# Recalibrating the planner of a static schedule: attention and a gated FFN on one core, with the softmax's exponentials shared by two engines

## The chip, the core and the metric

The kernel runs on one core of a Trainium2 chip. The core has five engines that run side by side, each through its own list of instructions in order: TensorE (PE, matrix products), ScalarE (ACT, here the exponentials), VectorE (DVE, elementwise work), GpSimd (POOL) and SyncE (SP, which here only issues DMA transfers). They tell each other of finished work through semaphores. Matrix products land in PSUM, which has eight banks of 128 x 512 float32; everything else lies in SBUF. The metric is the time of one execution on the device, in microseconds; the median of several runs is given.

## The reference

One transformer block with attention and FFN in parallel on the normalised input: 2048 positions, width 512, 32 heads of 16, FFN width 1792.

```python
x = A_x
xn = _layernorm(x, axis=-1)
return x + _A_ref(xn, A_wqkv, A_wo) + _B_ref(xn, B_w1, B_w3, B_w2)

# _A_ref: attention, Dh = 16
scores = jnp.einsum("bhqd,bhkd->bhqk", q, k) * (Dh ** -0.5)
p = _softmax(scores, axis=-1)
o = jnp.einsum("bhqk,bhkd->bhqd", p, v)
return (lambda x, *d: x.transpose(*d))(o, 0, 2, 1, 3).reshape(B, S, D) @ wo

# _B_ref: gated FFN
h = _silu(gate) * up
out = jnp.einsum("bsf,fd->bsd", h, w2)
```

With 32 heads of 16, the scores have 32 x 2048 x 2048 elements for little matrix work, so the exponentials are the large item.

## The kernel before

**Units, ranks, chunks.** Attention is cut into 32 units (`NU`): four blocks of 512 queries times eight groups of four heads. A unit has 64 ranks (`RPU`): 16 key tiles of 128 times four heads. Scores are made two ranks at a time, that is in chunks of 128 x 1024, 32 to a unit and 1024 in all (`score`, L1673: two matmuls that use two of the array's four row groups).

**Two ways to an exponential.** A chunk goes to ACT or to DVE. On ACT it is one instruction (`try_a`, L1716): exp from PSUM banks 0 and 1, or 2 and 3, into one of ten slots of PT. On DVE (`try_d`, `chain`) it goes by integer arithmetic on the bits of a bfloat16. p1 (L1768) clamps the scores of banks 4 and 5 into a slot of y as int16. Then, for one chunk or a pair of chunks together, m (L1807) takes the mantissa, g (L1823) subtracts a constant, t (L1814) multiplies y by m, and e (L1828) masks y in place. The exponential is the sum of e, g and t, and it is P·V that adds them: a DVE chunk gives three P·V terms where an ACT chunk gives one. There are three slots of y, two of m (t overwrites m) and two of g. A slot comes free when P·V has read it.

**P·V and dense work.** P·V (`try_pv`, L1882) works in column mode, four heads side by side, and adds into bank 7 for one unit at a time, in the order of the units. When a unit is complete, DVE copies bank 7 out (`unit_end`, L1900) and a small chain of DMAs and DVE or POOL work normalises it. Everything else on PE is "dense" work in column mode: projections, FFN and output (L1301), in tiles that use bank 6 alone in the long middle stage. Each FFN tile needs ACT for a tanh (L1462) and DVE for two products (L1466, L1476).

**The planner.** No order is written by hand. `_plan_fast` runs a small event simulation in Python when the kernel is built. Time `P.t` goes on in steps of 0.02 us; at each step every free engine takes the posted piece with the lowest priority number whose time has come (`post`, `pump`), and PE takes the first that fits of: a chunk for ACT, a chunk for DVE, dense work (while the P·V backlog is under `PVQ` tasks), P·V, dense work. What it takes is appended to that engine's list, and those lists are the program. The durations are formulas (`a_cost`, `d_cost`, `s_cost`, and numbers at single pieces); a result counts as ready `_LAT` after its end. So the share of chunks that DVE gets, and all order, come from the model's times. On the chip only the order and the semaphores remain: an engine waits until its next instruction's inputs are there, whatever the planner thought.

**Dependencies.** `_collect` finds, by keys, what an instruction must wait for: the last writer of what it reads, and the last writer and the readers of what it writes. `_finish` drops those on PE itself; on DVE and ACT an instruction does wait, by semaphore, for an earlier one of its own engine. The slots of y, m and g lie where x was, so p1, m and g name all 16 keys of x (`XD`) among their writes.

**DVE chunks at a unit's end.** `try_d` takes the next rank in order. It takes none past rank 52 of a unit (`D_LAST`), and past rank 42 (`D_PAIR`) it makes chains of one chunk. Ranks go alternately to the two halves of the row groups (`dpar`). p1 of the next pair waits until the chain before has done two of its four steps (first chunk) or four (second).

Of the kernel before, what the change touches and what calls it, by code (L numbers as in the profile page):

```python
# [20 lines left out]
class _Prog:  # L21
# [7 lines left out]

    def _collect(self, op, reads, writes):  # L30
# [22 lines left out]
        deps.pop(id(op), None)  # L53
        return list(deps.values())
# [15 lines left out]
    def op(self, eng, fn, reads=(), writes=(), name="", first=None):  # L70
# [7 lines left out]
        deps = self._collect(op, reads, writes)  # L78
        return self._finish(op, deps)
# [58 lines left out]
_LAT = 0.09  # L138


class _Sched(_Prog):


    def __init__(self):
# [5 lines left out]
        self.ring = 0.0  # L150

    def _time(self, op, deps, dur, tail):
        ready = self.t
# [5 lines left out]
        start = max(self.free[op.eng], ready)  # L159
        op.end = start + dur + tail  # L160
        self.free[op.eng] = start + dur
        return op

    def op(self, eng, fn, reads=(), writes=(), dur=0.1, name=""):
        op = _Prog.op(self, eng, fn, reads, writes, name)
        return self._time(op, op.deps, dur, 0.18 if eng == "pe" else 0.0)
# [828 lines left out]
def _plan_fast(nc, ps, flag, A_x, A_wqkv, A_wo, B_w1, B_w3, B_w2, out):  # L995
# [18 lines left out]
    NP = NG // 2  # L1014
    NY = 3
    NM = 2
# [5 lines left out]
    D_PAIR = RPU - 22  # L1022
    D_LAST = RPU - 12
    NW = 3
    PVQ = 8
# [10 lines left out]
    with ctx:  # L1036
# [59 lines left out]
        XD = [("x", t) for t in range(NT)]  # L1096
        def xk(s0, n):
# [86 lines left out]
        def norm(t):  # L1184
# [4 lines left out]
                     reads=[("x", t), ("lnr", n0), ("mv", t)], writes=[("xn", xs)], dur=0.25)  # L1189
# [4 lines left out]
        def stat(ts, prio):  # L1194
# [3 lines left out]
            def one(t):  # L1198
                nrm0[t] = t0
                P.op("dve", lambda e: e.bn_stats(stats[:, t, :], x_sb[:, t, :]),  # L1200
                     reads=[("x", t)], writes=[("st", t)], dur=0.64)
# [45 lines left out]
        P.post("dve", wv_check, ready=60.0, prio=4)  # L1247

        def tail_consts():
# [15 lines left out]
            P.post("dve", tail_masks, ready=P.free["pool"] + _LAT, prio=4)  # L1265
# [303 lines left out]
        st = {"dbl": 0, "pos": 0, "pv": 0, "dpar": 0, "nd": 0, "lastA": -1.0, "n_exp": 0, "pm": ("col", None, 0.0)}  # L1569
# [74 lines left out]
        def pe_dur(mode, rows=None):  # L1644
            lm, lr, lt = st["pm"]
            if mode == "row":
                if lm == "row":
                    d = 0.04 if lr is not None and lr != rows and lt >= P.t - 0.05 else 0.22
                    rows = None if d < 0.1 else rows
                else:  # L1650
                    d = 0.32
            else:
                d = 0.218 if lm == "col" else 0.318
            st["pm"] = (mode, rows, P.t + d)
            return d

        def score(b0, name):
            r0 = st["pos"]
            u, rr = divmod(r0, RPU)
            kt, j0 = divmod(rr, 4)  # L1660
# [14 lines left out]
            o = P.op("pe", f, reads=rd, writes=[("ps", b0), ("ps", b0 + 1)], dur=pe_dur("row", j0),  # L1675
                     name="%s%d" % (name, r0))
            st["pos"] += 2
            return r0, u, j0, kt, o
# [5 lines left out]
        def try_a():  # L1684
# [15 lines left out]
            x = score(2 * buf, "A")  # L1700
            if x is None:
                return False
            r0, u, j0, kt, o = x
# [33 lines left out]
        def try_d():  # L1737
            r0 = st["pos"]
            if r0 >= NR or st["early"] or not idle((4, 5)) or dbuf[0] > P.t:
# [7 lines left out]
            r0, u, j0, kt, o = x  # L1747
            st["dpar"] ^= 2
# [5 lines left out]
            if sl is None:  # L1754
                sl = dcur[0] = {"y": None, "n": 0, "ch": [], "done": 0, "max": 2 if rr <= D_PAIR else 1}
# [7 lines left out]
            def p1():  # L1763
                if sl["y"] is None:
# [4 lines left out]
                                                          0.0, 32767.0, ALU.max, ALU.min),  # L1769
                         reads=[("ps", 4), ("ps", 5)], writes=[("ds", ys)] + XD, dur=1.215, name="p1")  # L1770
                dbuf[0] = q.end + _LAT
                if last:
# [5 lines left out]
            need = 2 if c == 0 else 4  # L1778
# [3 lines left out]
            return True  # L1782

        def chain(sl):
# [3 lines left out]
            y = dsl[:, ys, 0:n]  # L1788
            b = {}

            def give(k, arr, ap, q_, pool):
# [6 lines left out]
                for c, (u, j0, kt) in enumerate(sl["ch"]):  # L1798
                    st["n_exp"] += (k == 0) * 2
                    for i in range(2):  # L1800
                        add_task(u, j0 + i, kt, ap[:, 1024 * c + 512 * i:1024 * c + 512 * i + 512].bitcast(BF16),
                                 q_.end + _LAT, ("ds", arr[0]), rel)

            def f_m():
# [4 lines left out]
                     reads=[("ds", ys)], writes=[("ds", NY + m_)] + XD, dur=s_cost(n), name="m")  # L1809

            def f_t():
# [4 lines left out]
                          reads=[("ds", ys)], writes=[("ds", NY + m_)], dur=0.175 + 0.00052 * n, name="t")  # L1816
                give(2, (NY + m_, m_), t_ap, q_, mfree)

            def f_g():
# [3 lines left out]
                q_ = P.op("dve", lambda e: e.tensor_scalar(g_ap, y, -352.0, 0.0, ALU.add, ALU.max),  # L1823
                          reads=[("ds", ys)], writes=[("ds", NY + NM + g_)] + XD, dur=s_cost(n), name="g")
# [380 lines left out]
```

## Time and profile before

| | us |
|---|---|
| median of the runs | 840.64 (839.43 to 847.51, three runs) |
| the profiled execution | 838.6 |
| its span, first to last instruction | 836.6 |
| first exponential of attention starts | 17.2 |
| last one ends | 819.8 |

The profile is of one execution. A row of a group gives its line, engine, operation, tiles and count; then the time in which at least one of them ran, the mean duration of one in ns, and the idle time of the engine just before them with what ended most of it. Durations on DVE and ACT run from an instruction's start until its result is written; the next one, when it waits for nothing, starts before that. Ends of matmuls are modelled.

### The profile page before, as it was taken

The page shows a single profiled execution, that of the slowest core. Times are in us where ns is not written, and L with a number is a line of the kernel's source. Part 1 is how long each engine was busy: PE and PEld are TensorE (multiplying, and loading weights), DVE is VectorE, ACT ScalarE, POOL GpSimd, SP SyncE. Part 2 cuts the span into 40 slices and gives each one's busy share as a digit, 9 for nine tenths or more (in the row PEclk, how much of TensorE's full clock was granted, in tenths as well). Part 3 has the DMA queues.
Part 4 walks back from the last instruction along what each step waited for, and adds up shares of the span by engine and source line. Part 5 has one row for each costly group of instructions (what it writes and reads, how often), then busy time and mean ns, then how long its engine had stood idle before and what let it go on. Part 6 is the DMA issues. An engine that isn't in the chain of part 4 may idle for free.

```text
span 836.6 us, 20690 instructions
## 1 busy us (share of the span) xinstructions
PE 769.8 (92%) x8825; PEld 221.7 (27%) x8825; DVE 743.4 (89%) x978; ACT 797.9 (95%) x899; POOL 44.8 (5%) x54
## 2 busy tenths in 40 slices
PE   7999998988999988899999989999999889999996
PEld 4432222222222222222222222222222222222222
DVE  8759998999999888989989999899998899989981
ACT  5999999999999999999999999999998999999982
POOL 4500100000000000000000010000000010000000
PEclk9999999999999999999999999999999999999988
DMA  5126343133222322343221423332112333312220
GB/s 176 46 69 129 34 59 39 30 56 34 33 35 33 53 33 46 33 58 41 27 22 31 58 30 47 45 52 34 12 30 39 46 53 39 40 35 15 26 15 31
DMA packets 88782, 36.95 MB, mean 44 GB/s; under 512 B 73192, under 2 KB 85096, under 8 KB 88680
## 3 DMA queue, kind: packets, MB, share of 16 engines
q1 hardware_dynamic: 88680, 35.53, 28.9%
q8 instruction: 71, 1.16, 0.6%
q14 instruction: 31, 0.25, 0.1%
HBM read 22.81 MB, written 2.10 MB: 30 GB/s over the span
## 4 chain that ended last, share of the span: by engine, by line
ACT 60%; PE 20%; DVE 15%; DMA 2%; issue 1%; SPq 0%; POOL 0%; DVEq 0%; ACTq 0%; POOLq 0%
ACT f_PT L1716 57%; PE ps L1301 8%; PE ps L1673 6%; PE ps L1882 5%; DVE f_xd L1768 5%; ACT f_th L1462 3%; DVE f_xd L1814 2%; DVE f_xd L1823 1%; DVE f_xd L1807 1%; DVE f_xd L1828 1%; DMA f_R<-f_Rrow 1%; DVE f_hT L1476 1%; DVE f_stats L1200 1%; DVE f_xn_sb L1187 1%; DVE f_t L1466 1%
## 5 line engine op out<-in xcount | busy, mean ns | idle before, releaser
L1716 ACT ACTIVATE f_PT<-ps 128x1024 bf16<-128x1024 f32 x819 | 769.4, 1104 | 13.1 <-PE ps L1673 12.6
L1673 PE MATMUL ps<-f_QT,f_KT 32*128 32x512 bf16 x2048 | 326.8, 387 | 31.8 <-ACT f_PT L1716 26.6
L1768 DVE TENSOR_SCALAR f_xd<-ps 128x1024 int16<-128x1024 f32 x205 | 250.2, 1220 | 25.5 <-PE ps L1673 18.4
L1882 PE MATMUL ps<-f_PT,f_Vaug 128*32 128x512 bf16 (+1 forms) x1638 | 222.7, 388 | 2.6 <-DVE f_xd L1828 1.1
L1882 PE MATMUL ps<-f_xd,f_Vaug 128*32 128x512 bf16 (+1 forms) x1230 | 177.5, 389 | 8.8 <-DVE f_xd L1823 3.4
L1673 PEld LDWEIGHTS ps<-f_QT,f_KT 32*128 32x128 bf16 x2048 | 82.5, 91 | 344.6 <-ACT f_PT L1716 298.9
L1301 PE MATMUL ps<-f_xnT,f_w 128*32 128x512 bf16 x1792 | 148.0, 383 | 6.4 <-DVE f_t L1466 5.5
L1814 DVE TENSOR_TENSOR f_xd<-f_xd 128x2048 bf16<-128x2048 bf16 (+1 forms) x112 | 125.5, 1121 | 0.0
L1301 PE MATMUL ps<-f_w,f_hT 128*32 128x512 bf16 x896 | 79.0, 386 | 0.4 <-DVE f_wkv L1519 0.4
L1828 DVE TENSOR_SCALAR f_xd<-f_xd 128x2048 int16<-128x2048 int16 (+1 forms) x112 | 77.0, 687 | 2.3
L1882 PEld LDWEIGHTS ps<-f_PT,f_Vaug 128*32 128x32 bf16 (+1 forms) x1638 | 54.3, 91 | 83.4 <-issue 65.9
L1807 DVE TENSOR_SCALAR f_xd<-f_xd 128x2048 int16<-128x2048 int16 (+1 forms) x112 | 74.4, 665 | 2.0
L1823 DVE TENSOR_SCALAR f_xd<-f_xd 128x2048 int16<-128x2048 int16 (+1 forms) x112 | 73.2, 654 | 2.5
L1947 POOL TENSOR_TENSOR f_onorm<-f_U,f_R 128x512 bf16<-128x512 f32 x15 | 22.2, 1477 | 720.9 <-DMA f_R<-f_Rrow 621.6
L1882 PEld LDWEIGHTS ps<-f_xd,f_Vaug 128*32 128x32 bf16 (+1 forms) x1230 | 42.5, 92 | 57.7 <-issue 25.8
L1301 PEld LDWEIGHTS ps<-f_xnT,f_w 128*32 128x32 bf16 x1792 | 38.3, 94 | 54.3 <-issue 45.0
L1466 DVE SCALAR_TENSOR_TENSOR f_t<-f_th,ps 128x512 bf16<-128x512 f32 x56 | 38.0, 679 | 11.0 <-ACT f_th L1462 10.6
L1476 DVE SCALAR_TENSOR_TENSOR f_hT<-f_t,ps 128x512 bf16<-128x512 bf16 x56 | 38.2, 682 | 9.3 <-PE ps L1301 8.4
L1462 ACT ACTIVATE f_th<-ps 128x512 f32<-128x512 f32 x56 | 38.8, 693 | 0.0
L1301 PEld LDWEIGHTS ps<-f_w,f_hT 128*32 128x32 bf16 x896 | 20.2, 95 | 20.1 <-issue 14.5
L1301 PE MATMUL ps<-f_wo,f_onorm 128*32 128x512 bf16 x272 | 22.8, 400 | 2.0 <-POOL f_onorm L1947 1.3
L1301 PE MATMUL ps<-f_xnT,f_wq 128*32 128x512 bf16 x256 | 22.8, 383 | 0.1
(80 smaller groups left out, 243.6 us busy)
## 6 DMA issues: line engine op xcount, KB each, us to landing
f_w<-in_B_w_dram SPq DMA_DIRECT2D x112, 128.0 KB, 3.6
f_R<-f_Rrow SPq DMA_DIRECT2D x124, 32.0 KB, 4.3
f_xr<-in_A_x_dram SPq DMA_DIRECT2D x16, 128.0 KB, 3.3
out_dram<-f_xn_sb SPq DMA_DIRECT2D x16, 128.0 KB, 1.8
f_KT<-f_stg SPq DMA_DIRECT2D x31, 64.0 KB, 2.4
f_QT<-f_stg SPq DMA_DIRECT2D x31, 64.0 KB, 2.6
f_U<-f_U SPq DMA_DIRECT2D x60, 32.0 KB, 2.0
f_w<-in_B_w_dram SPq DMA_DIRECT2D x7, 256.0 KB, 5.0
```

Source lines behind the costliest of these rows:

```text
L1301: ins = e.matmul(bank(bk)[32 * i:32 * i + 32, 0:ncols], make_lhsT(i), rhs_ap, start=start, stop=stop, tile_position=(0, 32 * i))
L1462: q = P.op("act", lambda e: e.activation(th[:, ss, :], bank(bk), ACTF.Tanh, scale=0.5), reads=[("ps", bk)], writes=[("th", ss)], dur=a_cos ...
L1466: q2 = P.op("dve", lambda e: e.scalar_tensor_tensor(t1[:, ss, :], th[:, ss, :], 1.0, bank(bk), ALU.add, ALU.mult), reads=[("th", ss), ("ps ...
L1476: q = P.op("dve", lambda e: e.scalar_tensor_tensor(hT[:, fc, :], t1[:, ss, :], 0.5, bank(bk), ALU.mult, ALU.mult), reads=[("t1", ss), ("ps ...
L1673: ins = e.matmul(bank(b), l_, r_, start=True, stop=True, tile_position=(rp, 0))
L1716: q = P.op("act", lambda e: e.activation(PT[:, s_, :], ps[:, b0 * 512:(b0 + 2) * 512], ACTF.Exp, scale=ASC, bias=ABIAS), reads=[("ps", b0) ...
L1768: q = P.op("dve", lambda e: e.tensor_scalar(dsl[:, ys, 1024 * c:1024 * c + 1024], ps[:, 4 * 512:6 * 512], 0.0, 32767.0, ALU.max, ALU.min), ...
L1807: P.op("dve", lambda e: e.tensor_scalar(dsl[:, NY + m_, 0:n], y, 0x7F, 0x3F00, ALU.bitwise_and, ALU.bitwise_or), reads=[("ds", ys)], write ...
L1814: q_ = P.op("dve", lambda e: e.tensor_tensor(t_ap.bitcast(BF16), y.bitcast(BF16), t_ap.bitcast(BF16), ALU.mult), reads=[("ds", ys)], write ...
L1823: q_ = P.op("dve", lambda e: e.tensor_scalar(g_ap, y, -352.0, 0.0, ALU.add, ALU.max), reads=[("ds", ys)], writes=[("ds", NY + NM + g_)] + ...
L1828: q_ = P.op("dve", lambda e: e.tensor_scalar(y, y, 0x7F80, None, ALU.bitwise_and), reads=[], writes=[("ds", ys)], dur=s_cost(n), name="e")
L1882: ins = e.matmul(bank(PV)[32 * j:32 * j + (17 if g % 2 == 0 else 32), :], v_, p_, start=s0, stop=s1, tile_position=(0, 32 * j))
```

## The change

Five parts, all in the planner; the kernel's arithmetic stays, but for one constant.

- Dependencies: on DVE and ACT, a dependency on the same engine is kept only if the instruction reads what the other wrote. y gets a key for each 512 columns, and the keys of x are named only when a part of a slot is first written.
- Model: pitch (how long the engine is taken) and latency (until the result can be used) apart, one latency for each pair of engines, new duration formulas, and a model of PE with row and column mode (`pem`).
- DVE chunks: `a_next` and `d_next` choose them. DVE draws from the next unit once the current one has 10 chunks or fewer left, prefers row groups that the last score did not use, and always makes pairs, but for the last unit.
- Order: p1 of the next pair may follow one step (first chunk) or two steps (second) of the chain before; `PVQ` 8 becomes 20; PE holds other work back for 0.26 us after a score; the check of the weights and the masks of the tail go from priority 4 to 1.
- p1 clamps at 352 and not at 0 (`G_LO`), the same constant that g subtracts. Code that would give g to POOL in pieces is added, and switched off (`POOL_G = False`, so `gq` stays empty and `P.port` 0).

```diff
@@ _collect
+        raw = {id(reg[k][0]) for k in reads if k in reg}
...
+        if op.eng in self.ordered:
+            return [d for d in deps.values() if d.is_dma or d.eng != op.eng or id(d) in raw]
         return list(deps.values())
...
-_LAT = 0.09
+_LAT = 0.06
+_LATS = {("pe", "act"): 0.041, ("pe", "dve"): 0.053, ("dve", "pool"): 0.083, ("pool", "dve"): 0.033, ("act", "dve"): 0.033}
+_TAILS = {"act": 0.182, "dve": 0.083, "pool": 0.05, "sp": 0.0}
 class _Sched(_Prog):
+    ordered = ("dve", "act")
...
+    def _ready(self, op, deps):
+        ready = self.t - 0.03
         for d in deps:
-            if d.eng == op.eng and not d.is_dma:
-                ready = max(ready, d.end)
+            if d.is_dma:
+                l = 0.09
+            elif d.eng == op.eng:
+                l = 0.034
             else:
-                ready = max(ready, d.end + _LAT)
...
+                l = _LATS.get((d.eng, op.eng), 0.055)
+            ready = max(ready, d.end + l)
+        return ready
...
+        lm, lr, ls = self.pem
+        if mode == "row":
+            if lm == "row":
+                gap = 0.217 if rows & lr else 0.007
+            else:
+                gap = 0.318
+            start = max(ready, ls + gap)
...
+        elif mode == "col":
+            start = max(ready, ls + (0.217 if lm == "col" else 0.318))
@@ _plan_fast
+    G_LO = 352.0
+    POOL_G = False
-    D_PAIR = RPU - 22
-    D_LAST = RPU - 12
+    D_LEFT = 10
+    D_ONE = 11
+    D_STOP = 6
-    PVQ = 8
+    PVQ = 20
...
-        a_cost = lambda n: 0.095 + 0.000833 * n
-        d_cost = lambda n: 0.145 + 0.001045 * n
-        s_cost = lambda n: 0.18 + 0.000256 * n
+        a_cost = lambda n: 0.049 + 0.000834 * n
+        d_cost = lambda n: 0.054 + 0.00106 * n
+        s_cost = lambda n: 0.075 + 0.000261 * n
...
-        P.post("dve", wv_check, ready=60.0, prio=4)
+        P.post("dve", wv_check, ready=60.0, prio=1)
...
+        def d_next():
+            x = a_next()
+            if x is None:
+                return None
+            u, i = x
+            if left[u] <= D_LEFT and u + 1 < NU:
+                u += 1
+            elif u == NU - 1 and left[u] <= D_STOP:
+                return None
+            c = [i for i in range(RPU // 2) if not taken[u][i]][:2]
+            lm, lr, lt = P.pem
+            c.sort(key=lambda i: (lm == "row" and i % 2 * 2 in lr, i))
+            for i in c:
+                if st["dbal"] * (1 - i % 2 * 2) <= 2:
+                    return u, i
+            return None
...
-            rr = r0 % RPU
-            if rr > D_LAST or r0 % 4 != st["dpar"]:
-                return False
-            x = score(4, "D")
+            nx = d_next()
+            x = score(4, "D", *nx) if nx is not None else None
...
-                sl = dcur[0] = {"y": None, "n": 0, "ch": [], "done": 0, "max": 2 if rr <= D_PAIR else 1}
+                sl = dcur[0] = {"y": None, "n": 0, "ch": [], "done": 0, "max": 2 if u < NU - 1 or left[u] > D_ONE else 1}
...
-                                                          0.0, 32767.0, ALU.max, ALU.min),
-                         reads=[("ps", 4), ("ps", 5)], writes=[("ds", ys)] + XD, dur=1.215, name="p1")
+                                                          G_LO, 32767.0, ALU.max, ALU.min),
+                         reads=[("ps", 4), ("ps", 5)], writes=[("ds", ys, 2 * c), ("ds", ys, 2 * c + 1)] + xd_keys(ys, 1024 * c, 1024 * c + 1024), dur=d_cost(1024), name="p1")
...
-            need = 2 if c == 0 else 4
+            need = 1 if c == 0 else 2
...
             def f_e():
                 q_ = P.op("dve", lambda e: e.tensor_scalar(y, y, 0x7F80, None, ALU.bitwise_and),
-                          reads=[], writes=[("ds", ys)], dur=s_cost(n), name="e")
+                          reads=YK, writes=YK, dur=s_cost(n), name="e", lock=True)
...
-                    elif try_a() or try_d() or (backlog() < PVQ and st["pos"] < NR and try_dense()) or try_pv() or try_dense():
+                    elif try_a() or try_d() or ((P.pem[0] != "row" or P.t >= P.pem[2] + 0.26) and (
+                            (backlog() < PVQ and st["pos"] < NR and try_dense()) or try_pv() or try_dense())):
```

More of the change, by code (lines that the diff above doesn't have):

```diff
@@ L1642, in idle, with a_next, score @@
             return all(bank_free[b] <= P.t for b in bs) and not any(a.bank in bs for a in active)
[L1644 to L1660, printed above, removed]
+        taken = [[False] * (RPU // 2) for u in range(NU)]
+        left = [RPU // 2] * NU
+        st["ua"] = 0
+        def a_next():
+            while st["ua"] < NU and left[st["ua"]] == 0:
+                st["ua"] += 1
+            if st["ua"] >= NU:
+                return None
+            return st["ua"], taken[st["ua"]].index(False)
+        def d_next():
[13 more added lines that the diff above has]
+                    return u, i
+            return None
+        def score(b0, name, u, ix):
+            kt, j0 = ix // 2, ix % 2 * 2
+            r0 = u * RPU + 2 * ix
             g = u % NG
```

157 lines of the change are left out of this document (120 added, 37 removed).

## The prediction, made before the changed kernel was run

> **What bounds the kernel now.** I read the page first: its busy times, the chain that ended last and the costliest groups.
>
> ```profile
> span 836.6 us, 20690 instructions
> PE 769.8 (92%) x8825; PEld 221.7 (27%) x8825; DVE 743.4 (89%) x978; ACT 797.9 (95%) x899; POOL 44.8 (5%) x54
> ACT 60%; PE 20%; DVE 15%; DMA 2%; issue 1%; SPq 0%; POOL 0%; DVEq 0%; ACTq 0%; POOLq 0%
> ...
> L1716 ACT ACTIVATE f_PT<-ps 128x1024 bf16<-128x1024 f32 x819 | 769.4, 1104 | 13.1 <-PE ps L1673 12.6
> L1673 PE MATMUL ps<-f_QT,f_KT 32*128 32x512 bf16 x2048 | 326.8, 387 | 31.8 <-ACT f_PT L1716 26.6
> L1768 DVE TENSOR_SCALAR f_xd<-ps 128x1024 int16<-128x1024 f32 x205 | 250.2, 1220 | 25.5 <-PE ps L1673 18.4
> ...
> L1814 DVE TENSOR_TENSOR f_xd<-f_xd 128x2048 bf16<-128x2048 bf16 (+1 forms) x112 | 125.5, 1121 | 0.0
> ...
> L1828 DVE TENSOR_SCALAR f_xd<-f_xd 128x2048 int16<-128x2048 int16 (+1 forms) x112 | 77.0, 687 | 2.3
> ...
> L1807 DVE TENSOR_SCALAR f_xd<-f_xd 128x2048 int16<-128x2048 int16 (+1 forms) x112 | 74.4, 665 | 2.0
> L1823 DVE TENSOR_SCALAR f_xd<-f_xd 128x2048 int16<-128x2048 int16 (+1 forms) x112 | 73.2, 654 | 2.5
> ...
> f_QT<-f_stg SPq DMA_DIRECT2D x31, 64.0 KB, 2.6
> ```
>
> Three engines are near full, so the page alone does not name the bound. The busy time by stage does; its columns are PE, PEld, DVE, ACT, POOL, clock, DMA share and rate.
>
> ```profile
> 17.20:55.00 37.80, 35.95 (x520) 14.16 (x512) 24.15 (x48) 34.17 (x43) 12.65 (x15) 1.00 0.20 49
> 55.00:800.00 745.00, 695.02 (x7904) 190.87 (x7900) 690.37 (x874) 739.18 (x829) 24.94 (x22) 1.00 0.30 41
> 800.00:820.00 20.00, 18.05 (x166) 4.34 (x170) 12.44 (x15) 15.45 (x17) 0.00 (x0) 0.74 0.21 14
> 820.00:836.60 16.60, 8.67 (x123) 4.08 (x111) 3.05 (x10) 1.68 (x3) 0.00 (x0) 0.90 0.13 39
> ```
>
> From 55 to 800 us ACT is busy 739.18 of 745 us: it is the bound there. Its work is exponentials, 819 chunks (one chunk is two 128x512 score blocks) at 769.4 / 819 = 0.94 us each. The other 205 of the 1024 chunks go to DVE. ACT can therefore only get shorter in two ways: its own small waits shrink, or chunks move to DVE. DVE has 745 - 690.37 = 54.6 us of plain idle time in that stage, and what it loses inside its "busy" time is the next thing to look for. The table of waits says on what the engines sit idle (us in total, times, longest):
>
> ```profile
> DVE f_xd L1768 <- PE ps L1673: 18.4, 25, 3.0
> DVE f_t L1466 <- ACT f_th L1462: 10.6, 9, 2.1
> DVE f_hT L1476 <- PE ps L1301: 8.4, 16, 1.8
> ...
> DVE f_Vaug L1312 <- PE ps L1301: 7.1, 9, 1.7
> DVE f_onorm L1941 <- DMA f_R<-f_Rrow: 2.9, 1, 2.9
> ...
> ACT f_PT L1716 <- PE ps L1882: 0.2, 1, 0.2
> ```
>
> Then the timeline of DVE over one unit end (start, duration). The distance from one start to the next, not the duration, is what an instruction costs its engine.
>
> ```profile
> 404.40 0.68 DVE L1807 TENSOR_SCALAR f_xd<-f_xd 128x2048 int16<-128x2048 int16 x1
> 405.12 0.69 DVE L1823 TENSOR_SCALAR f_xd<-f_xd 128x2048 int16<-128x2048 int16 x1
> 405.92 1.23 DVE L1768 TENSOR_SCALAR f_xd<-ps 128x1024 int16<-128x1024 f32 x1
> 407.06 0.24 DVE L1920 RECIPROCAL f_Rc<-f_Lc 128x16 f32<-128x16 f32 x1
> 407.22 0.63 DVE L1390 TENSOR_SCALAR f_stg<-ps 128x512 bf16<-128x512 f32 x1
> 407.76 1.21 DVE L1814 TENSOR_TENSOR f_xd<-f_xd 128x2048 bf16<-128x2048 bf16 x1
> 409.00 0.69 DVE L1828 TENSOR_SCALAR f_xd<-f_xd 128x2048 int16<-128x2048 int16 x1
> 409.61 1.22 DVE L1768 TENSOR_SCALAR f_xd<-ps 128x1024 int16<-128x1024 f32 x1
> 410.86 0.69 DVE L1807 TENSOR_SCALAR f_xd<-f_xd 128x2048 int16<-128x2048 int16 x1
> 411.59 0.70 DVE L1823 TENSOR_SCALAR f_xd<-f_xd 128x2048 int16<-128x2048 int16 x1
> ```
>
> e (L1828) to the next p1 (L1768) takes 0.61 us, with no wait between them. m to g, the same kind of work on the same size, takes 0.72 and 0.73: g waits for the end of m. g to p1 takes 0.80. p1 to the reciprocal takes 1.14, but p1 to its own m 1.25. So a wait on the engine's own last instruction costs 0.11 to 0.19 us here.
>
> **The exchange rate.** A chunk costs DVE (250.2 + 125.5 + 77.0 + 74.4 + 73.2) / 205 = 2.93 us and ACT 0.94 us. When x us of DVE time come free and the planner hands out chunks until both engines are full again, n = x / (2.93 + 0.94) chunks move and the time falls by 0.94 n = 0.243 x. A microsecond of wait taken off ACT itself is worth 2.93 / 3.87 = 0.76 us. So DVE gains count a quarter, ACT gains or losses three quarters. I make the sum with x and an ACT term.
>
> **Waits between DVE instructions that share only a buffer.** `_collect` now keeps a dependency on the same engine only where something written is read. Three waits go from a pair's chain: g behind m (both wrote the 16 x keys), 0.115 us; p1 behind g (the same keys), 0.19; e behind t (e overwrites what t read), 1.24 - 1.13 = 0.11, where 1.13 is t's 1.21 less the 0.08 by which p1's 1.22 exceeds its free pitch of 1.14. Per pair 0.42 us. Twice 112 instructions less 205 gives 19 chunks alone and 93 pairs, so the ceiling is 93 x 0.42 = 39 us. In the stretch above all of these places pay, yet p1 and t show that other work often stands between two of the chain; I take 70%, 27 us. The floor is 0. m still waits for p1 and t for m, because they read.
>
> The Trainium skill, page "VectorE: DVE Perf Modes", section "The DRAIN you can't avoid", speaks against this term: it says that eight copies took 13.88 us with a semaphore after each and with one at the end alike, so that the wait costs nothing extra. By that rule the 27 us would be 0. The trace does not agree: 0.72 and 0.73 us against 0.61.
>
> **Pairs across unit ends.** `d_next` lets DVE draw from unit u+1 when unit u has 10 chunks or fewer left; before, it drew none in the last 6 of a unit. Of its idle time, 18.4 us in 25 waits are p1 waiting for a score, about one a unit, up to 3.0 us. I take 14 of these; what is late next is the chain's m, because the pairs of u+1 keep their slots (three y, two m, two g) until bank 7 is handed over. Floor 0, ceiling 18.4 plus the gaps filled by other work, some 30 in all. The chunks left single become pairs:
>
> ```profile
> L1814 DVE TENSOR_TENSOR f_xd<-f_xd 128x2048 bf16<-128x2048 bf16 x93 | 112.5, 1210 | 0.0
> ...
> L1828 DVE TENSOR_SCALAR f_xd<-f_xd 128x1024 int16<-128x1024 int16 x19 | 8.1, 425 | 0.5
> ```
>
> A 1024-wide e takes 0.425 us beside 0.687 at the mean; L1814's 19 narrow ones take (125.5 - 112.5) / 19 = 0.68 against 1.210 for twice the data. So a chunk alone costs (0.68 - 0.605) + 3 x (0.425 - 0.35) = 0.30 us more; 14 of 19 paired give 4 us. What a moved pair issues: two score groups earlier on PE, five DVE instructions, twelve P·V matmuls later; no DMA, and nothing is moved past SP or POOL. QT of the next unit must have landed, 2.6 us after its issue; its tile is due 60 ranks ahead of its unit and DVE asks 20 ranks ahead, 40 of the unit's 64 ranks later, some 16 us at 836.6 / 32 = 26 us a unit. That hides it; cost nothing.
>
> **The recalibrated planner.** The old model gave an exponential 0.948 us of pitch (0.095 + 0.000833 x 1024) and 0.09 us for every semaphore; the new one 0.903, with the latency apart. p1 goes from 1.215 to 1.139, near the 1.14 of the trace; m, g and e from 0.704 to 0.610, near 0.61. So the order written out is closer to when things are really ready. I credit it with a third of the 10.6 + 8.4 + 7.1 us that DVE waits for ACT and PE in the dense tiles: 8 us (bounds -8 to 20). On ACT, 13.1 us stand before exponentials; I take 3 away (bounds: all 10 that are not at the very end, or 20 more: next part).
>
> **The rest.** Score pairs of DVE are now chosen for the row groups that ACT's pair left free, and PE holds 0.26 us behind a score; P·V waits for a backlog of 20 tasks instead of 8. These move PE's work, whose gaps I count in the two terms above; 14 more DVE chunks bring 14 x 4 = 56 more matmuls, 14 groups of four, which at the new model's 0.217 us a group make 3 us of PE, covered by the 745 - 695 = 50 us in which PE is idle from 55 to 800 us. If that cover goes, it is 3 us. A backlog of 20 can fill the ten PT slots; an exponential waited for a slot once, 0.2 us, and I keep that. The weight check L1228 comes ahead of the chains: one instruction, DVE only, hidden by ACT. G_LO changes a constant, the finer keys end in the same instructions, and the POOL pieces are off (`POOL_G` False): nothing. No wait is added. The start (17.2 us) and the end keep their place: the 2.9 us for which DVE waits for R, once, near the end, is a DMA whose model is not touched, and I leave the clock of 0.74 from 800 to 820 us as it is.
>
> **Sum.** x = 27 + 14 + 4 + 8 = 53 us; n = 53 / 3.87 = 14 chunks; 0.94 x 14 = 13 us. ACT's own term: 3 x 0.76 = 2. Together 15 us off the profiled execution's 838.6 us: 823. That execution is 2 us under the median of the three runs, 840.64 (839.43 to 847.51), so I put the next median 1 us higher: 824.
>
> **Rivals.**
> Waits that cost nothing (the skill's rule): x = 26, 6.3 + 2.3 us, 830. The rows speak against it. Chance 0.07.
> More than forecast: x to 95 (39 + 30 + 6 + 20) and 10 us off ACT: 23 + 8, 808. For it: ACT's whole middle stage hangs on the number of chunks. Against: DVE would have to be without idle time. Below 815, 0.17.
> No change: slots of the next unit's pairs hold DVE where PE held it, so terms two and four go, x = 31, 7.5 us; and scores come 9 us late in all, 7 us back: 838. For it: the slots are as few as before. Against: three y slots serve a pair each 745 / 100 = 7 us. Chance 0.15.
> Slower: the old pitch of 0.948 left PE's order 0.045 us of cushion per exponential; the new one leaves none, and PE, busy 695 of 745 us, must change between score and P·V mode for each. If one exponential in three waits 0.15 us longer for L1673, that is 805 / 3 x 0.15 = 40 us, x 0.76 = 30 us: 838.6 - 15 + 30 = 854. It decides from 15 / 0.76 = 20 us of new ACT waits, 25 ns an exponential. Against: today PE waits 26.6 us for ACT at L1673, twice what ACT waits for PE there (12.6), so PE has been early more often than late. Chance 0.11.
>
> **How the numbers follow.** Forecast 0.50 (its own range 815 to 832), more 0.17, the rule 0.07, no change 0.15, slower 0.11. Faster by over 1% (about what a measurement of this kernel can tell from no change) means under 832.2: 0.50 + 0.17 + 0.05 = 0.72. Within 1%: 0.02 + 0.15 = 0.17. Slower 0.11. The range, 806 to 842, leaves out about 0.05 below and 0.12 above.
>
> **What would show it.** L1716 near x805 and L1768 near x219; L1814 to L1828 near x112 again, nearly all of them 2048 wide. g behind m at 0.61 and e behind t at 1.13 in the timeline; if they stay at 0.72 and 1.24, the first term was wrong. L1768's wait for L1673 below 6 us; if instead DVE idles before L1807, the slots hold it. L1716's idle time near 10 us, with the busy time per exponential at 0.94 or under; if it passes 30 us, the slower rival is on. The prediction is wrong if the count of L1716 hardly falls, or if the end after the last exponential grows beyond today's 16.6 us.

## The result, and the profile after

| | before | after |
|---|---|---|
| median, us | 840.03 (837.27 to 847.51) | 814.69 (813.22 to 817.97) |
| ratio | | 0.969, 95% interval 0.962 to 0.976 |
| profiled execution, us (span) | 838.6 (836.6) | 814.2 (812.3) |
| chunks on ACT / on DVE | 819 / 205 | 794 / 230 |

The changed kernel is faster by 25 us. In one run below (the model alone, 870.3 us) the clock was lower than in its other runs, and its ratio leaves that run out. The page of the kernel after, with the same parts as before (L1788 is the exponential on ACT, L1742 the scores, L1837 p1, L1893 m, L1909 g, L1900 t, L1950 e):

```profile
span 812.3 us, 20816 instructions
PE 775.6 (95%) x8925; PEld 224.6 (28%) x8925; DVE 775.1 (95%) x1015; ACT 776.0 (96%) x874; POOL 44.1 (5%) x54
...
L1788 ACT ACTIVATE f_PT<-ps 128x1024 bf16<-128x1024 f32 x794 | 746.4, 1091 | 9.9 <-PE ps L1742 9.1
L1742 PE MATMUL ps<-f_QT,f_KT 32*128 32x512 bf16 x2048 | 331.0, 385 | 14.1 <-ACT f_PT L1788 7.1
L1837 DVE TENSOR_SCALAR f_xd<-ps 128x1024 int16<-128x1024 f32 x230 | 278.6, 1211 | 1.6 <-PE ps L1742 1.2
...
L1900 DVE TENSOR_TENSOR f_xd<-f_xd 128x2048 bf16<-128x2048 bf16 x115 | 142.1, 1235 | 0.0
L1909 DVE TENSOR_SCALAR f_xd<-f_xd 128x2048 int16<-128x2048 int16 x115 | 81.2, 706 | 0.0
L1893 DVE TENSOR_SCALAR f_xd<-f_xd 128x2048 int16<-128x2048 int16 x115 | 79.4, 691 | 0.6 <-PE ps L1356 0.2
L1950 DVE TENSOR_SCALAR f_xd<-f_xd 128x2048 int16<-128x2048 int16 x115 | 79.0, 687 | 0.0
```

ACT works no faster: 746.4 / 794 is 0.94 us an exponential, as before. It has 25 fewer, and 25 x 0.94 = 23.5 us is nearly the whole gain of 24.4 in the profiled executions. All chains are pairs now (x115, one form). Where DVE found the time shows in the busy time from 55 to 775 us (PE, PEld, DVE, ACT, POOL). Before, in the sum of that stretch:

```profile
sum 720.00, PE 670.13 PEld 184.12 DVE 666.93 ACT 714.18 POOL 23.41; mean PE 335.07 PEld 92.06 DVE 333.47 ACT 357.09 POOL 11.71
```

and after:

```profile
55.00:775.00 720.00, 701.00 (x8020) 194.07 (x8016) 714.74 (x900) 715.36 (x803) 24.05 (x22) 1.00 0.31 44
775.00:797.00 22.00, 18.95 (x184) 4.58 (x180) 16.67 (x23) 19.08 (x21) 0.00 (x0) 0.82 0.17 8
797.00:812.30 15.30, 9.71 (x129) 4.41 (x121) 3.04 (x10) 1.79 (x3) 0.00 (x0) 0.83 0.14 42
```

DVE's plain idle time in the 720 us fell from 53 to 5 us; ACT stands where it stood. The table of waits says which ones went. Those for p1 (18.4), the tanh (10.6) and the dense products (8.4) are all but gone; those of the first 50 us (L1367) and the one for R near the end are not:

```profile
DVE f_Vaug L1367 <- PE ps L1356: 7.0, 10, 1.7
...
DVE f_onorm L2069 <- DMA f_R<-f_Rrow: 2.5, 1, 2.5
...
DVE f_xd L1837 <- PE ps L1742: 1.2, 3, 0.6
...
DVE f_hT L1531 <- PE ps L1356: 0.5, 2, 0.2
...
DVE f_t L1521 <- ACT f_th L1517: 0.3, 1, 0.3
```

The timeline of DVE in the kernel after shows how the chains now run. Two chains lie in one another: t, m, e, p1 and then g, with no two neighbours of which one reads what the other wrote, and steps of 0.60 to 0.61 us for m, e and g and 1.13 to 1.14 for t and p1.

```profile
402.25 1.22 DVE L1837 TENSOR_SCALAR f_xd<-ps 128x1024 int16<-128x1024 f32 x1
403.39 1.22 DVE L1900 TENSOR_TENSOR f_xd<-f_xd 128x2048 bf16<-128x2048 bf16 x1
404.52 0.68 DVE L1893 TENSOR_SCALAR f_xd<-f_xd 128x2048 int16<-128x2048 int16 x1
405.13 0.69 DVE L1950 TENSOR_SCALAR f_xd<-f_xd 128x2048 int16<-128x2048 int16 x1
405.73 1.22 DVE L1837 TENSOR_SCALAR f_xd<-ps 128x1024 int16<-128x1024 f32 x1
406.86 0.68 DVE L1574 TENSOR_TENSOR f_wkv<-ps,f_xr 128x512 f32<-128x512 f32 x1
407.46 0.68 DVE L1909 TENSOR_SCALAR f_xd<-f_xd 128x2048 int16<-128x2048 int16 x1
408.06 1.22 DVE L1837 TENSOR_SCALAR f_xd<-ps 128x1024 int16<-128x1024 f32 x1
```

### The profile page after: what moved, and what is told of

Read it like the earlier page. It is cut to its first block, busy times and chain, and to the rows that moved or that the text cites. A ratio compares the mean times of both kernels' runs of the same rounds, so it can differ in the third digit from the quotient of the medians.

```text
span 812.3 us, 20816 instructions
## 1 busy us (share of the span) xinstructions
PE 775.6 (95%) x8925; PEld 224.6 (28%) x8925; DVE 775.1 (95%) x1015; ACT 776.0 (96%) x874; POOL 44.1 (5%) x54
## 4 chain that ended last, share of the span: by engine, by line
ACT 50%; PE 24%; DVE 19%; DMA 3%; issue 2%; POOL 1%; SPq 1%; DVEq 0%; POOLq 0%
ACT f_PT L1788 48%; PE ps L1356 9%; PE ps L1742 8%; DVE f_xd L1837 6%; PE ps L2010 6%; ACT f_th L1517 3%; DVE f_xd L1900 3%; DVE f_xd L1909 2%; DVE f_xd L1950 2%; DVE f_xd L1893 2%; DMA f_R<-f_Rrow 2%; DMA f_Rrow<-f_Rc 1%; DVE f_hT L1531 1%; SPq L2058 1%; DVE f_t L1521 1%
## 5 line engine op out<-in xcount | busy, mean ns | idle before, releaser
L1788 ACT ACTIVATE f_PT<-ps 128x1024 bf16<-128x1024 f32 x794 | 746.4, 1091 | 9.9 <-PE ps L1742 9.1
L1742 PE MATMUL ps<-f_QT,f_KT 32*128 32x512 bf16 x2048 | 331.0, 385 | 14.1 <-ACT f_PT L1788 7.1
L1837 DVE TENSOR_SCALAR f_xd<-ps 128x1024 int16<-128x1024 f32 x230 | 278.6, 1211 | 1.6 <-PE ps L1742 1.2
L2010 PE MATMUL ps<-f_PT,f_Vaug 128*17 128x512 bf16 (+1 forms) x1588 | 211.0, 386 | 0.3 <-DVE f_xd L1900 0.3
L2010 PE MATMUL ps<-f_xd,f_Vaug 128*17 128x512 bf16 (+1 forms) x1380 | 191.5, 387 | 3.5 <-DVE f_xd L1950 2.6
L1742 PEld LDWEIGHTS ps<-f_QT,f_KT 32*128 32x128 bf16 x2048 | 83.5, 91 | 328.6 <-ACT f_PT L1788 277.2
L1900 DVE TENSOR_TENSOR f_xd<-f_xd 128x2048 bf16<-128x2048 bf16 x115 | 142.1, 1235 | 0.0
L1909 DVE TENSOR_SCALAR f_xd<-f_xd 128x2048 int16<-128x2048 int16 x115 | 81.2, 706 | 0.0
L1893 DVE TENSOR_SCALAR f_xd<-f_xd 128x2048 int16<-128x2048 int16 x115 | 79.4, 691 | 0.6 <-PE ps L1356 0.2
L1950 DVE TENSOR_SCALAR f_xd<-f_xd 128x2048 int16<-128x2048 int16 x115 | 79.0, 687 | 0.0
L2010 PEld LDWEIGHTS ps<-f_PT,f_Vaug 128*17 128x17 bf16 (+1 forms) x1588 | 50.6, 92 | 54.4 <-issue 44.7
L2010 PEld LDWEIGHTS ps<-f_xd,f_Vaug 128*17 128x17 bf16 (+1 forms) x1380 | 46.2, 92 | 54.7 <-issue 30.4
L2028 DVE COPY f_U<-ps 128x512 f32<-128x512 f32 x31 | 21.1, 679 | 0.4 <-PE ps L2010 0.3
```

Source lines behind the costliest of these rows:

```text
L1742: ins = e.matmul(bank(b), l_, r_, start=True, stop=True, tile_position=(rp, 0))
L1788: q = P.op("act", lambda e: e.activation(PT[:, s_, :], ps[:, b0 * 512:(b0 + 2) * 512], ACTF.Exp, scale=ASC, bias=ABIAS), reads=[("ps", b0) ...
L1837: q = P.op("dve", lambda e: e.tensor_scalar(dsl[:, ys, 1024 * c:1024 * c + 1024], ps[:, 4 * 512:6 * 512], G_LO, 32767.0, ALU.max, ALU.min) ...
L1893: P.op("dve", lambda e: e.tensor_scalar(dsl[:, NY + m_, 0:n], y, 0x7F, 0x3F00, ALU.bitwise_and, ALU.bitwise_or), reads=YK, writes=[("ds", ...
L1900: q_ = P.op("dve", lambda e: e.tensor_tensor(t_ap.bitcast(BF16), y.bitcast(BF16), t_ap.bitcast(BF16), ALU.mult), reads=YK + [("ds", NY + m ...
L1909: q_ = P.op("dve", lambda e: e.tensor_scalar(g_ap, y, -G_LO, 0.0, ALU.add, ALU.max), reads=YK, writes=[("g", g_, k) for k in range(n // 51 ...
```

## The experiments

Every run was timed beside the kernel before on the same chip, whose median lay between 837.7 and 839.7 us; ratios are to it. The changed kernel was not timed again there, so what is said to lie over its 814.7 us is a comparison across chips. For the two runs with the waits back and for p1 after two and four steps the ratio's interval meets or overlaps that of the changed kernel (0.962 to 0.976); their 5 to 6 us are the best figures there are, and no more. The runs with limits of 12, 13 and 18 also give the check of the softmax sums a buffer of its own; in the run of the model alone with limit 8 that check waits for two FFN slots as well.

| run | median, us (range) | ratio to before, 95% interval | exponentials on ACT |
|---|---|---|---|
| before's lists, no such waits | 832.0 (829.8 to 835.7) | 0.993 (0.990 to 0.996) | 819 |
| after's lists, waits back | 821.1 (820.8 to 822.1) | 0.981 (0.975 to 0.987) | 794 |
| waits back and planned | 820.0 (818.7 to 824.1) | 0.980 (0.973 to 0.986) | 796 |
| no draw across unit ends | 827.7 (822.3 to 828.5) | 0.989 (0.983 to 0.994) | 802 |
| p1 after two and four steps | 819.7 (816.7 to 823.0) | 0.976 (0.971 to 0.981) | 797 |
| old durations | 839.1 (834.8 to 841.2) | 0.999 (0.996 to 1.001) | 805 |
| old durations, backlog 12 | 825.7 (825.1 to 826.2) | 0.986 (0.983 to 0.989) | 805 |
| model alone, backlog 8 | 859.4 (855.0 to 870.3) | 1.028 (1.020 to 1.035) | 808 |
| model alone, backlog 13 | 827.3 (825.7 to 829.0) | 0.987 (0.984 to 0.990) | 808 |
| waits planned, backlog 8 | 865.9 (864.1 to 867.0) | 1.034 (1.027 to 1.040) | 793 |
| R later in the plan | 811.2 (810.6 to 812.2) | 0.966 (0.962 to 0.970) | 794 |
| R later, backlog 18 | 808.2 (807.6 to 811.2) | 0.966 (0.963 to 0.969) | 793 |

**The price of a wait, orders held fixed.** In two runs the five lists stay instruction for instruction, and only the waits differ. The kernel before without them:

```diff
-        op.deps = deps
+        op.planned, op.deps = deps, (deps := [d for d in deps if d.is_dma or d.eng != op.eng or id(d) in op.raw] if isinstance(self, _Sched) and op.eng in ("dve", "act") else deps)
...
-        return self._time(op, op.deps, dur, 0.18 if eng == "pe" else 0.0)
+        return self._time(op, op.planned, dur, 0.18 if eng == "pe" else 0.0)
```

Here `op.raw` holds the writers of what the instruction reads, and the planner's times go on using all dependencies. t now also names its slot of m among its reads, and e its slot of y, so that both keep the waits for what they read.

> The kernel before, its lists unchanged, with the waits between VectorE (and ScalarE) instructions that only share a buffer left out. Theory 1: g behind m in 0.61 instead of 0.73 us, but the 819 exponentials of ScalarE stay, so VectorE only idles longer before p1 and in the dense tiles, and the time hardly moves: 834 to 840, the count of chunks being what sets it. Theory 2 (waits cost nothing): 838 and g behind m still at 0.73. Theory 3 (late VectorE work holds up TensorE and ScalarE directly): 815 to 828.

The timeline of DVE in that run, at the unit end shown of before:

```profile
403.15 0.69 DVE L1807 TENSOR_SCALAR f_xd<-f_xd 128x2048 int16<-128x2048 int16 x1
403.75 0.69 DVE L1823 TENSOR_SCALAR f_xd<-f_xd 128x2048 int16<-128x2048 int16 x1
404.35 1.22 DVE L1768 TENSOR_SCALAR f_xd<-ps 128x1024 int16<-128x1024 f32 x1
...
406.35 1.22 DVE L1814 TENSOR_TENSOR f_xd<-f_xd 128x2048 bf16<-128x2048 bf16 x1
407.48 0.69 DVE L1828 TENSOR_SCALAR f_xd<-f_xd 128x2048 int16<-128x2048 int16 x1
```

m to g takes 0.60 (0.72 with the wait), g to p1 0.60 (0.80), t to e 1.13 (1.24): the prices of the prediction, within 0.01. The rule of the Trainium skill (page "VectorE: DVE Perf Modes", section "The DRAIN you can't avoid") that such a wait costs nothing does not hold in this kernel. Over the whole timeline g stands right behind m 73 times, p1 behind g 57 times and e behind t 53 times, and the shorter steps there free 25 us of DVE. The time fell by 7 us although no chunk moved, which none of the three expectations had. The row of the exponentials shows one way:

```profile
L1716 ACT ACTIVATE f_PT<-ps 128x1024 bf16<-128x1024 f32 x819 | 767.8, 1116 | 7.0 <-PE ps L1673 6.9
```

ACT's idle time before exponentials fell from 13.1 to 7.0 us. A late DVE also holds PE's list up, and through it the next score; my exchange rate had left that way out. PE's idle time before the P·V terms of DVE's chunks shows it, in the kernel before and in this run:

```profile
L1882 PE MATMUL ps<-f_xd,f_Vaug 128*32 128x512 bf16 (+1 forms) x1230 | 177.5, 389 | 8.8 <-DVE f_xd L1823 3.4 <-DVE f_xd L1814 3.1 <-DVE f_xd L1828 2.0
L1882 PE MATMUL ps<-f_xd,f_Vaug 128*32 128x512 bf16 (+1 forms) x1230 | 175.8, 385 | 3.1 <-DVE f_xd L1823 1.4 <-DVE f_xd L1814 0.9
```

The other direction, the changed kernel with its lists and the waits back:

```diff
-        if op.eng in self.ordered:
-            return [d for d in deps.values() if d.is_dma or d.eng != op.eng or id(d) in raw]
+        op.raw = raw
         return list(deps.values())
...
-        return self._time(op, op.deps, dur, _TAILS[eng])
+        planned = [d for d in op.deps if d.is_dma or d.eng != op.eng or eng not in self.ordered or id(d) in op.raw]
+        return self._time(op, planned, dur, _TAILS[eng])
...
-            if a >= lo and b <= hi:
+            if a > b:
                 return []
```

The filter now serves the planner's times alone, and p1, m and g name the keys of x each time.

> The changed kernel's lists, instruction for instruction, with the waits on the own engine put back (m, g and p1 name the keys of x again, and anything that shares a buffer waits); the planner does not know of them. Theory 1 (a wait on the engine's own last instruction costs 0.11 to 0.19 us of pitch, and VectorE is full now): up to 115 x 0.42 = 48 us more VectorE work in an order that cannot hand chunks back, so 835 to 860 us with still 794 exponentials on ScalarE, and m to the next in 0.72 rather than 0.60 us. Theory 2 (the waits cost nothing): 812 to 817.

It cost 6.4 us, not 20 to 45. The pitches say why. In this run m to p1 takes 0.79 us,

```profile
432.22 0.68 DVE L1893 TENSOR_SCALAR f_xd<-f_xd 128x2048 int16<-128x2048 int16 x1
433.01 1.23 DVE L1837 TENSOR_SCALAR f_xd<-ps 128x1024 int16<-128x1024 f32 x1
```

and in the changed kernel 0.60:

```profile
428.07 0.68 DVE L1893 TENSOR_SCALAR f_xd<-f_xd 128x2048 int16<-128x2048 int16 x1
428.67 1.22 DVE L1837 TENSOR_SCALAR f_xd<-ps 128x1024 int16<-128x1024 f32 x1
```

That is the one place that still pays: 70 times 0.19 us, 13 us of DVE's time. In the interleaved order g stands behind m once and e behind t once, so nearly everywhere else a wait finds its work done. My 0.42 us a pair belonged to the old order. When the planner knows of the waits the result is the same within the ranges (the edit of `xd_keys` is as above):

```diff
-    ordered = ("dve", "act")
+    ordered = ()
```

> The changed kernel with the same waits put back as in the first run, and the planner knows of them, so that it plans a new order with fewer VectorE chunks. Theory 1: 48 us of VectorE time at 0.25 to 0.27 each, +12 us: 823 to 831 with 805 to 810 exponentials on ScalarE. Theory 2: 812 to 817 and 794.

5 us, less than the 8 to 16 expected; it changed the count by two only.

**The draw across unit ends.**

```diff
-            if left[u] <= D_LEFT and u + 1 < NU:
-                u += 1
-            elif u == NU - 1 and left[u] <= D_STOP:
+            if left[u] <= D_STOP:
                 return None
...
-                sl = dcur[0] = {"y": None, "n": 0, "ch": [], "done": 0, "max": 2 if u < NU - 1 or left[u] > D_ONE else 1}
+                sl = dcur[0] = {"y": None, "n": 0, "ch": [], "done": 0, "max": 2 if left[u] > D_ONE else 1}
```

> The changed kernel, but VectorE draws no chunk from the next unit: none in the last 6 chunks of a unit and chains of one chunk from 11 on, as before the change. Theory 1 (the draw fills the hole at each unit end): 30 to 45 us of VectorE time lost, +8 to +12 us: 821 to 828 with 803 to 807 exponentials on ScalarE, and VectorE waits for scores before p1 again (10 to 20 us). Rival (the recalibrated planner fills the hole with other work): 812 to 817.

```profile
L1788 ACT ACTIVATE f_PT<-ps 128x1024 bf16<-128x1024 f32 x802 | 754.0, 1068 | 9.1 <-PE ps L1742 7.9 <-PE ps L2010 0.3
...
L1837 DVE TENSOR_SCALAR f_xd<-ps 128x1024 int16<-128x1024 f32 x222 | 270.0, 1216 | 18.4 <-PE ps L1742 17.8
```

By its groups of instructions the run has p1's wait for scores back, 17.8 us (18.4 before the change), and the eight chunks at 0.94 us make 7.5. The median is 13 us over the changed kernel. The runs spread over 6 us, and the profiled one was the fastest, 822.3, 8 us over. The other four show a mean granted clock of TensorE of 0.966 to 0.968 against its 0.983; where in the run they lost it was not profiled. The earlier p1 is smaller:

```diff
-            need = 1 if c == 0 else 2
+            need = 2 if c == 0 else 4
```

> The changed kernel, but p1 of the next pair waits for two and four steps of the chain before, as in the kernel before, not for one and two. Theory 1 (the early p1 puts other work between m and its neighbours and frees banks 4 and 5 sooner): VectorE idles 10 to 25 us more before p1 and m waits for p1 again, 817 to 823 us with 797 to 803 exponentials. Rival (no effect, since the chains give enough cover): 812 to 817.

5 us and three chunks, with ranges that overlap the changed kernel's. DVE's wait before p1 hardly rose, so the expected 10 to 25 us of it did not come; that m waits for p1 again did:

```profile
403.06 1.21 DVE L1837 TENSOR_SCALAR f_xd<-ps 128x1024 int16<-128x1024 f32 x1
404.31 0.69 DVE L1893 TENSOR_SCALAR f_xd<-f_xd 128x2048 int16<-128x2048 int16 x1
```

The step is 1.25 us and not 1.14, and it occurs 74 times, 8 us of DVE's time; in the changed kernel it occurs three times. g stands behind m 77 times again and e behind t 69 times. So it is the earlier p1 that lays two chains in one another, and this order takes away a wait for work that is read, which dropping dependencies can't.

**The durations.** The old formulas in the new planner:

```diff
-        a_cost = lambda n: 0.049 + 0.000834 * n
-        d_cost = lambda n: 0.054 + 0.00106 * n
-        s_cost = lambda n: 0.075 + 0.000261 * n
+        a_cost = lambda n: 0.095 + 0.000833 * n
+        d_cost = lambda n: 0.145 + 0.001045 * n
+        s_cost = lambda n: 0.18 + 0.000256 * n
...
-                          reads=YK + [("ds", NY + m_)], writes=[("ds", NY + m_)], dur=0.068 + 0.00052 * n, name="t", lock=True)
+                          reads=YK + [("ds", NY + m_)], writes=[("ds", NY + m_)], dur=0.175 + 0.00052 * n, name="t", lock=True)
```

> The changed kernel with the old duration formulas in the planner alone (an exponential 0.948, p1 1.215, m, g and e 0.704, t as before); all else of the change stays. Theory 1 (an order planned with the true pitch is what keeps VectorE busy): the planner hands VectorE fewer chunks, 810 or more exponentials on ScalarE, VectorE waits again in the dense tiles, 822 to 832 us. Rival (the old pitch was a useful cushion): ScalarE waits less for scores than the 9.1 us of the changed kernel, and 806 to 816 us.

The whole gain was gone, more than the 11 more exponentials can cost (10 us). The busy time by stage of that run (PE, PEld, DVE, ACT, POOL, then the clock) shows the rest:

```profile
760.00:780.00 20.00, 19.21 (x110) 3.49 (x110) 15.00 (x19) 15.66 (x16) 0.00 (x0) 0.50 0.04 10
...
800.00:822.00 22.00, 21.04 (x130) 4.17 (x132) 16.95 (x24) 18.61 (x19) 0.00 (x0) 0.50 0.17 8
```

TensorE's granted clock stood at 0.50 in two stretches of some 20 us, in which ACT was idle for 4.3 and 3.4 us. In this plan the FFN's products were done by 748 us, and from 754 to 822 us PE had scores, P·V and ten other matmuls. So I ran the old durations with a backlog limit that spreads dense work to the end:

```diff
-    PVQ = 20
+    PVQ = 12
```

> The run with the old durations again, but with the backlog limit at 12, so that dense work lasts until the last scores and TensorE is not left half idle from 750 us on (its clock stood at 0.50 for some 40 us there). Theory 5 (of the 24 us that the old durations cost, some 10 are the 11 exponentials that VectorE did not take, the rest the fallen clock): 820 to 829 us with 803 to 808 exponentials and a clock of 0.98 or more. Rival (the old durations cost it all by a poorer order): 834 to 840.

```profile
55.00:775.00 720.00, 686.06 (x7748) 190.28 (x7740) 679.34 (x850) 716.47 (x800) 21.86 (x21) 1.00 0.31 43
775.00:800.00 25.00, 24.89 (x294) 6.88 (x296) 21.90 (x28) 24.98 (x28) 1.28 (x1) 1.00 0.18 19
```

825.7 us with the same 805 exponentials, and a clock of 1.00. The durations are worth some 11 us, in 11 chunks (the limit, 12 and not 20, differs too): DVE is idle 720 - 679 = 41 us here and 5 in the changed kernel. What the old plan took to be a full DVE was not one.

**The model alone, and the backlog.** Waits, draw and earlier p1 undone together (the edits above), and `PVQ` at 8. With the model stay the choice of row groups, PE's hold of 0.26 us and the priorities:

> The changed kernel with the other parts undone together: waits on the own engine back and known to the planner, no draw from the next unit and single chunks at its end, p1 after two and four steps, P·V from a backlog of 8. What is left is the recalibrated model with the choice of row groups. By the sum of the single runs so far (5 us for the waits, 10 for the draw, a few for the rest) 830 to 834 us, against 839 for the kernel before: so the model alone is worth 5 to 9. If the parts cover for each other (undoing one alone shows less than it is worth), 835 or more; if the model is the main part, 820 to 829.

That was slower than the kernel before, though its last exponential starts at 805 us against 819. Its last stretch:

```profile
806.00:852.80 46.80, 38.69 (x615) 19.86 (x615) 17.59 (x31) 6.57 (x11) 0.00 (x0) 0.91 0.23 57
```

47 us of tail, in which PE makes 615 matmuls and ACT has all but nothing to do: dense work that was left over. With the limit at 13:

> The run of the model alone again (waits planned, no draw from the next unit, p1 after two and four steps), but with the backlog limit at 13, where the dense products end some 46 of 2048 score blocks ahead of the last, as in the changed kernel (30). Theory 4: the 859 us came from dense work left over, and without it the model alone gives 822 to 832 us, more than half of the 25 us. Rival (the model needs the other parts): 835 or more.

827.3 us, with 808 exponentials as well. So the model with what stays beside it, and with a backlog that lets dense work finish, has 11 of the 25 us, and the 859 came from the limit. One more run confirms it from the side of the changed kernel (the limit at 8 with the waits back and planned, 820 us at 20; for the limit of 8 in the changed kernel with nothing else altered there is no time):

> The run with the waits back and planned (820 us), with one more number changed: the backlog limit at 8 and not 20. Theory 4 (dense work has one bank in the middle stage and must end with the exponentials; the limit of 20 is what lets it): the last exponential comes at 790 to 804 us, and dense products of the last block are left for after it: a tail of 35 to 60 us instead of 15, 835 to 855 us. Theory 1 as predicted (the limit brings and costs nothing): 816 to 824.

865.9 us, 46 more. From its groups of instructions between 802 and 865 us:

```profile
L1356 PE MATMUL ps<-f_xnT,f_w 128*32 128x512 bf16 x392 | 26.1, 425 | 10.6 <-DMA f_w<-in_B_w_dram 10.6
L1356 PE MATMUL ps<-f_w,f_hT 128*32 128x512 bf16 x224 | 12.3, 379 | 0.7 <-DVE f_t L1521 0.7
```

392 of the 1792 FFN matmuls and all 224 of the last block's output products come after the exponentials, and wait 10.6 us for weights whose loads are started tile by tile. The backlog limit decides when dense work ends, and both sides cost: too low and it is left over, too high and PE runs half empty before the end and its clock falls.

**A better tail.** In the changed kernel PE waits 2.3 us for DVE near 787 us, behind the wait for R. One number in the plan moves that piece of DVE work behind the last pairs:

```diff
-                    P.post(eng, lambda: e5(eng), ready=q.end + _LAT, prio=0, cond=lambda: u // 2 < NON or all(
+                    P.post(eng, lambda: e5(eng), ready=q.end + _LAT + (2.6 if u == NU - 2 else 0.0), prio=0, cond=lambda: u // 2 < NON or all(
```

> The changed kernel with one time in the planner set later by 2.6 us: that at which R is there for the last but one unit's normalisation on VectorE. In the changed kernel VectorE waits 2.5 us there with e and t of the last pairs behind it, TensorE waits 2.3 us for g, and its clock falls. Theory 1: VectorE's wait and TensorE's go, the granted clock stays above 0.9 until the last exponential, 808 to 812 us. Rival (the tail is hidden behind the exponentials anyway): 813 to 817.

811.2 us, 3.5 less, with ranges that do not touch. The stages from 785 to 795 us of the changed kernel:

```profile
785.00:790.00 5.00, 2.54 (x24) 0.62 (x20) 3.52 (x5) 3.15 (x5) 0.00 (x0) 0.89 0.07 6
790.00:795.00 5.00, 4.95 (x32) 0.90 (x30) 4.25 (x6) 4.21 (x5) 0.00 (x0) 0.50 0.00 0
```

and of this run:

```profile
785.00:790.00 5.00, 3.76 (x38) 1.02 (x34) 4.84 (x7) 5.00 (x7) 0.00 (x0) 0.93 0.00 0
790.00:795.00 5.00, 5.00 (x44) 1.38 (x40) 1.05 (x2) 2.80 (x3) 0.00 (x0) 0.50 0.00 0
```

ACT is full to 790 us, but the clock falls all the same. With the limit at 18 as well:

> The changed kernel with the later time for R (811.2 us by itself) and the backlog limit at 18, so that dense products end 8 of 2048 score blocks ahead of the last one and not 30. Theory 5: TensorE stays busy to the end, its clock falls later or not at all, 805 to 810 us. Rival (what dense work gains before the last exponential it loses after it): 810 to 816.

```profile
785.00:790.00 5.00, 5.00 (x62) 1.30 (x58) 5.00 (x9) 5.00 (x6) 0.00 (x0) 1.00 0.12 31
790.00:795.00 5.00, 5.00 (x62) 2.49 (x64) 2.59 (x5) 2.01 (x3) 0.00 (x0) 1.00 0.00 0
```

The clock holds through the last exponential, and 808.2 us is the fastest of all. The kernel before also ran 2 us faster beside it, and the ratio is the same 0.966, so the second step is shown in the stages and not settled in the time. Both runs beat both kernels' medians.

## Why the prediction came out as it did

The way and the place were right: ACT bound, DVE time freed, chunks moved at 0.94 us each. 814.69 us lies in the range of 806 to 842, but below the forecast of 824 and just below that forecast's own range, 815 to 832; the count of 794 exponentials lies below the 805.

**The exchange rate** held as to chunks. Four runs lie within 2 us of a line of 0.94 us a chunk: 794 exponentials at 814.7, 805 at 825.7, 808 at 827.3, 819 at 840.0. The runs with 796, 797 and 802 lie 2 to 6 us above it, the two with a better tail 3 to 6 us below, and those with dense work at the wrong time far off. It missed one way: waits also reach ACT through PE's list, 7 us in the kernel before with no chunk moved.

**x was mis-sized: 53 us, and 95 by the chunks that moved.** 25 chunks at (660.3 / 230 + 0.94) = 3.81 us make 95, where 660.3 is the sum of DVE's five groups after. Of these, 48 us are the idle time of the middle stage, 25 the three waits of the prediction, and 6 the wait of m for p1 (58 times 0.11 in the kernel before), which the prediction had left standing; the rest stays open. The failed term is that of the recalibrated planner, 8 us for a third of the waits for ACT and PE. The 19.0 us of them in the FFN tiles fell to 0.8, the 7.1 at L1312 lie in the first 50 us and stayed, p1's wait fell from 18.4 to 1.2, and the durations are worth some 11 us of time, not 2. I had the numbers for it: 0.704 against 0.61 for 336 instructions, 1.215 against 1.14 for 205 and 1.24 against 1.13 for 93 come to 57 us which the old plan thought DVE busy and which it was not, where the waits on its own engine did not eat them.

**The waits** were priced right, each (0.11 to 0.19) and in sum: 25 us of DVE's time in the kernel before, 28 with the chunks left single, where the prediction took 27. Putting them back costs 6.4 us, and 27 x 0.243 = 6.6, but that agreement is luck: in the new order one place pays, 13 us in all, and on fixed lists no chunk moves.

**The unit ends** were too small: 14 + 4 us of x, 4.4 us of time; undone, some 8 us in the fastest run. The slots, named as what would be late next, do not hold m: its idle time is 0.6 us.

**ACT's own term** was right in size: 13.1 us before exponentials became 9.9, 3 taken.

**"Moves PE's work", for the backlog limit, was wrong.** I priced it by PT slots and looked for no date by which dense work has to end. It decides 46 us in one run and the sign of the change in another. In the kernel before, dense work used its one bank to the end, and the profile had shown it: output tiles still ran in the last 20 us.

**The end** was right: the wait for R (2.9, now 2.5 us) and the fallen clock stayed, and could be had for 3.5 us.

**The rivals.** "More than forecast" (808, chance 0.17) came: the time is below 815, x is the 95 that it named, and DVE is all but without idle time in the middle stage, the very thing held against it. Only ACT's own term, 3 us and not 10, kept the time above 808. The Trainium skill's rule fell by the pitches. The slots and the lost cushion did not come: ACT's wait for scores fell from 12.6 to 9.1 us.

## What to carry to other kernels

Where a planner deals work out between engines, an overstated duration is idle time of that engine, and it can be counted ahead as (planned pitch less measured pitch) x count, with the pitch taken from start to start and the latency kept apart: here 57 us of DVE, which at 0.243 are 14 us of time, against some 11 measured. Before a priority is changed, ask for each class of work by when it must be done, and what keeps the engine busy if it is done early. Parts undone one at a time can add up to more than the whole (5, 13, 5 and 24 of 25 us here), because undoing one can also move the end of other work: of the 24 us with the old durations, 13 went with the backlog limit. Where a cost can be tried on fixed lists, that gives its price in that order alone.

## What the runs showed of the hardware

TensorE's clock fell without a long pause. In the run with R later, PE's waits in the timeline from 783 to 789 us are

```profile
783.48 0.40 PE L1742 MATMUL ps<-f_QT,f_KT 32*128 32x512 bf16 x4 [0.53 <-ACT f_PT L1788]
...
787.14 0.39 PE L1742 MATMUL ps<-f_QT,f_KT 32*128 32x512 bf16 x2 [0.53 <-ACT f_PT L1788]
788.77 0.39 PE L2010 MATMUL ps<-f_PT,f_Vaug 128*32 128x512 bf16 x2 [0.32 <-DVE f_xd L1950]
```

the longest of them: none is over 0.53 us, PE is busy 3.76 of the 5 us from 785 us on, and then the clock is 0.50. The Trainium skill (page "TensorE: Matmul & The Clock Gate", section "Part 1: The HAM clock gate") gives an idle window of about 3.4 us as the condition; here PE had no such pause. Nor did a PE that is counted nearly full bring the clock back at once: with the old durations it stayed at 0.50 from 760 to 780 us with matmuls counted busy for 19.2 of 20 us, and it was at 1.00 again from 790 to 795. What share of idle time makes it fall or rise these runs do not settle.
